# Moving one batch's transposes from TensorE to the DMA crossbar in a sparse attention and MLP kernel

## The chip, the cores and the metric

The kernel runs on one core of a Trainium2 chip. The metric is device time in microseconds (us) of one execution. A run whose time is over 1.5% above the fastest of the same kernel is called slow, and "faster" or "slower" is said from 2% on. A ratio below is the mean time of one kernel's fast runs over that of the other's fast runs of the same rounds, so it is not quite the ratio of the medians that are quoted beside it. Intervals are 95%.

## The reference, cut to what matters

Eight batches of eight heads, 576 positions, 64 columns. Heads 0 to 3 see a window of 32 positions ("local"), heads 4 to 7 every 32nd position ("strided"). The attention output is the input of a two-layer network, 4608 tokens by 512, then 2048, then 512.

```python
mask_local   = (rel >= 0) & (rel < stride)
mask_strided = (rel >= 0) & (pos[None, :] % stride == pos[:, None] % stride)
...                                    # softmax(q k^T / 8) v for each head
h = x @ w_in
g = np.where(h > 0.0, h, np.exp(np.minimum(h, 0.0)) - 1.0)
return g @ w_out
```

## The kernel before

Scores need q and k with the 64 columns across partitions, so both are transposed. Two ways are in the kernel: TensorE against an identity matrix, with a copy out of PSUM after it (`piece_T`), or a DMA crossbar transpose queued on SyncE (`dma_T`). Before, batches 0 to 2 go the first way, batches 3 to 7 the second.

```python
def piece_T(b, hp, engs=None, wide=True):       # TensorE way
    ...
                nc.tensor.transpose(o, x, identity[0:n, 0:n])
    for i, (dst, blk) in enumerate(both):
        copy(engs[i] if engs else nc.vector, dst, ps[i])

def dma_T(b, which):                            # crossbar way
    ...
    nc.sync.dma_start_transpose(out=out_.rearrange("p (c n) -> p c n", n=n), in_=in_)
```

There is one pair of source tiles `qs`, `ks` for the strided heads of every batch: loads of the next batch wait until this batch is transposed. All loads but the first four, of batch 0, stand in GpSimd's queue, and the output stores in SyncE's.

After two blocks of layer 1, a hand-written order interleaves batch 1's attention with layer 2 groups (four matmuls each, `2` in the string). Then a loop over the remaining layer 1 groups carries everything else. `SC` says at which step each head pair's scores come; `u` is a half of it.

```python
for it in ("2 S4 2 S5 2 2 B4 S6 2 E4 A5 S7 2 E5 B6 2 E6 A7 2 E7 v "
           "T0 2 S0 S1 2 T1 k B0 2 E0 S2 2 A1 E1 S3 2 B2 E2 2 A3 2 E3 t 2 x").split():
    ...      # S scores, A/B probability times v, E its tail, T TensorE transposes of batch 1,
             # t those of batch 2's strided heads, v k x loads
for b in range(3, B):
    st = int(SC[b][0])
    ...
    at(st - (3 if b == 3 else 4), lambda b=b: Ts(b))          # crossbar, four tiles
for n, (j, t) in enumerate(L1S):
    for f in jobs.pop(n, []): f()
    l2_to(n + 10)
    for f in jobs.pop(n + .5, []): f()
    l1(j, t, mode="B" if n < 18 and n % 3 == 0 else "A")
```

The softmax here doesn't subtract the row's maximum and nothing guards it: scores larger than these inputs give would overflow.

## Time and profile before

| | before |
|---|---|
| time, median of the 4 runs beside the changed kernel | 324.17 us (323.82 to 325.11) |
| span of the profiled run | 322.6 us |
| TensorE idle from 24.78 to 94.72 us | 4.2 us |
| TensorE idle from 94.72 to 300 us | 0.14 us |

The page's first lines, the table of stretches and the rows of the timeline are shown and read in the prediction.

### The profile page before, as it was taken

How to read it: one execution, taken by the hardware profiler on the slowest of the kernel's cores; microseconds unless marked ns; L12 is line 12 of the kernel's file. 1: busy time of each engine (PE TensorE's matmuls, PEld its weight loads, DVE VectorE, ACT ScalarE, POOL GpSimd, SP SyncE). 2: the span in 40 equal slices, each digit the busy share in tenths (PEclk: the TensorE clock that was granted, in tenths of full speed). 3: DMA queues.
4: the chain of work that ended last, by engine and by line, in shares of the span. 5: the costliest groups of instructions: out<-in, count | busy, mean ns of one | idle time of the engine just before them, and what ended most of it. 6: DMA issues, size and time to landing. Idle time of an engine off the chain costs nothing.

```text
span 322.6 us, 7819 instructions
## 1 busy us (share of the span) xinstructions
PE 310.8 (96%) x2992; PEld 223.6 (69%) x2992; DVE 239.5 (74%) x485; ACT 220.2 (68%) x429; POOL 115.6 (36%) x162
## 2 busy tenths in 40 slices
PE   7898998989999999999999999999999999999994
PEld 5658953577667777777777777777777777777763
DVE  7664973477667888888888988898888866666660
ACT  3697766677688888777777777778888643443431
POOL 6352368788046903790259125920000000000000
PEclk9999999999999999999999999999999999999999
DMA  8999999999499949993999599969211111111112
GB/s 160 191 205 207 208 151 142 153 147 129 52 143 182 122 70 155 172 141 64 137 158 161 70 136 167 149 77 169 57 35 35 34 35 33 34 35 49 51 33 65
DMA packets 113990, 36.36 MB, mean 113 GB/s; under 512 B 101154, under 2 KB 107458, under 8 KB 113954
## 3 DMA queue, kind: packets, MB, share of 16 engines
q0 software_dynamic: 79696, 18.87, 61.3%
q1 hardware_dynamic: 32766, 16.28, 24.6%
q10 hardware_dynamic: 1492, 0.74, 1.0%
q8 instruction: 23, 0.38, 0.5%
q14 instruction: 13, 0.11, 0.1%
HBM read 38.04 MB, written 9.44 MB: 147 GB/s over the span
## 4 chain that ended last, share of the span: by engine, by line
PE 83%; DVE 6%; ACT 5%; DMA 3%; issue 1%; SPq 0%; DVEq 0%; ACTq 0%
PE ops L463 36%; PE hps L406 33%; PE sc L293 4%; PE ox L345 3%; DVE g L421 2%; DMA kl<-in_k_dram 2%; DMA ksT<-ks 1%; PE idle L487 1%; DVE g L440 1%; PE opl L478 1%; PE tp L270 1%; DVE he L420 1%; ACT vsx L528 1%; ACT big L437 1%; ACT e L296 1%
## 5 line engine op out<-in xcount | busy, mean ns | idle before, releaser
L463 PE MATMUL ops<-w_out_sb,g 128*128 128x512 bf16 x560 | 143.6, 380 | 0.1
L406 PE MATMUL hps<-xT,w_in_sb 128*128 128x256 bf16 x1088 | 140.7, 273 | 1.3 <-DVE g L421 1.3
L406 PEld LDWEIGHTS <-w_in_sb 128*128 128x128 bf16 x1088 | 117.3, 114 | 23.6 <-issue 1.5
L413 ACT ACTIVATE he<-hps 128x512 f32<-128x512 f32 x136 | 80.2, 593 | 52.3 <-PE hps L406 50.0
L421 DVE TENSOR_TENSOR g<-he,hps 128x512 bf16<-128x512 bf16 x130 | 89.4, 687 | 13.6
L463 PEld LDWEIGHTS <-g 128*128 128x128 bf16 x560 | 50.4, 98 | 37.2 <-DVE g L421 0.3
L420 DVE TENSOR_SCALAR he<-he 128x512 bf16<-128x512 f32 x130 | 57.7, 444 | 20.9 <-ACT he L413 19.5
L296 ACT ACTIVATE e<-sc 128x576 bf16<-128x576 f32 (+1 forms) x64 | 38.5, 645 | 4.6 <-PE sc L293 4.6
L468 ACT COPY osb<-ops 128x512 f32<-128x512 f32 x35 | 20.5, 587 | 12.3 <-PE ops L463 9.4
L143 POOL DMA_DIRECT2D qs<-in_q_dram x8 | 6.2, 774 | 48.9 <-DMA qsT<-qs 47.5
L348 ACT ACTIVATE ln<-ox 64x288 f32<-64x288 f32 x40 | 16.3, 409 | 10.7 <-PE ox L345 10.1
L125 POOL DMA_DIRECT2D klb<-in_k_dram x28 | 20.7, 747 | 7.9 <-DMA w_in_sb<-in_moe_w_in_dram 5.2
L133 POOL DMA_DIRECT2D vlx<-in_v_dram x28 | 21.9, 782 | 4.1 <-DMA w_out_sb<-in_moe_w_out_dram 1.9
L313 DVE TENSOR_TENSOR xT<-ox,rc 64x288 bf16<-64x288 f32 x40 | 18.1, 453 | 5.7 <-ACT rc L351 5.4
L317 DVE TENSOR_TENSOR xT<-ox,rc 64x288 bf16<-64x288 f32 x40 | 18.1, 453 | 5.5 <-ACT rc L351 5.1
L119 POOL DMA_DIRECT2D qlb<-in_q_dram x20 | 16.6, 833 | 13.8 <-DMA ks<-in_k_dram 10.0
L134 POOL DMA_DIRECT2D vlx<-in_v_dram x28 | 17.3, 618 | 4.2 <-DMA qlb<-in_q_dram 2.1
L351 ACT ACTIVATE rc<-ln 128x288 f32<-128x288 f32 x40 | 17.7, 443 | 1.3
L138 POOL DMA_DIRECT2D vsx<-in_v_dram x20 | 16.2, 816 | 0.9 <-DMA klb<-in_k_dram 0.9
L349 ACT ACTIVATE ln<-ox 64x288 f32<-64x288 f32 x40 | 16.1, 403 | 0.5
L304 DVE TENSOR_TENSOR pm<-e,mask_l 128x576 bf16<-128x576 bf16 x32 | 13.5, 453 | 3.3 <-ACT e L296 3.0
L487 PE MATMUL idle<-warm 128*128 128x256 bf16 x92 | 14.3, 299 | 1.3 <-DVE warm L182 1.3
(101 smaller groups left out, 243.2 us busy)
## 6 DMA issues: line engine op xcount, KB each, us to landing
out_dram<-osb SPq DMA_DIRECT2D x31, 144.0 KB
qs<-in_q_dram POOLq DMA_DIRECT2D x8, 288.0 KB, 6.4
ks<-in_k_dram POOLq DMA_DIRECT2D x8, 288.0 KB, 8.7
w_in_sb<-in_moe_w_in_dram POOLq DMA_DIRECT2D x2, 1024.0 KB, 17.0
w_out_sb<-in_moe_w_out_dram POOLq DMA_DIRECT2D x4, 512.0 KB, 15.7
klb<-in_k_dram POOLq DMA_DIRECT2D x28, 72.0 KB, 8.2
vlx<-in_v_dram POOLq DMA_DIRECT2D x28, 72.0 KB, 3.6
qlb<-in_q_dram POOLq DMA_DIRECT2D x20, 72.0 KB, 7.0
```

What stands on the lines that cost most here:

```text
L125: nc.gpsimd.dma_start(out=klb[b % 2][:, h // 2, :, (h % 2) * D:(h % 2 + 1) * D], in_=k[b, h].rearrange("(t p) d -> p t d", p=LQ))
L133: nc.gpsimd.dma_start(out=t[PRE:128], in_=x)
L296: nc.scalar.activation(e[0:R], sc[0:R, :, 0:W], ACT.Exp, scale=scale)
L313: nc.vector.tensor_mul(xs[:, u * W:(u + 1) * W], o[pr], rc[pr])
L317: nc.vector.tensor_mul(dst, o[pr].rearrange(pat, b=3, s=NS), rc[pr].rearrange(pat, b=3, s=NS))
L351: nc.scalar.activation(rc, ln, ACT.Exp, scale=-1.0)
L406: nc.tensor.matmul(hps[:, mm], lhsT=w_in_of(m, c), rhs=xT[:, c, r0:r0 + SUB], start=(c == 0), stop=(c == KC - 1))
L413: nc.scalar.activation(e, hps, ACT.Exp)
L420: eng.tensor_scalar(e1, e, scalar1=1.0, scalar2=1.0, op0=ALU.min, op1=ALU.subtract)
L421: nc.vector.tensor_tensor(gt, e1, hps, op=ALU.max)
L463: nc.tensor.matmul(ops, lhsT=g[:, m, kk * 128:(kk + 1) * 128], rhs=w_out_sb[:, m, :], start=(m == 0), stop=(m == MC - 1))
L468: nc.scalar.copy(o_sb, ops)
```

## The change

The intent is to spare TensorE all transposes of batch 2 and to close three waits in batch 1's attention. The core of the diff:

```diff
     def load_ql16(b):
-        if b < 3:
-            nc.gpsimd.dma_start(out=qld[b % 2][0:RS], ...)     # one load, halves apart
-            return
         for h in range(HG):                                    # four small loads
...
+    for i in range(2):                 # now at the empty start
+        one_columns(i)
     load_str(0, qs, q)
...
     def pitch(b):
-        return RS if b < 3 else RP
+        return RS if b < 2 else RP
...
-    one_columns(1)
     load_str(1, qs, q)
...
     load_str(2, ks, k)
-    load_kl16(2)
-    load_ql16(2)
-    load_vl16(2)
...
-    for it in ("2 S4 2 S5 2 2 B4 S6 2 E4 A5 S7 2 E5 B6 2 E6 A7 2 E7 v "
-               "T0 2 S0 S1 2 T1 k B0 2 E0 S2 2 A1 E1 S3 2 B2 E2 2 A3 2 E3 t 2 x").split():
+    for it in ("2 S4 2 S5 2 2 B4 S6 2 E4 A5 S7 2 E5 B6 2 E6 T0 2 t A7 v E7 S0 2 T1 S1 2 k B0 2 E0 S2 2 A1 E1 S3 t B2 2 "
+               "E2 A3 E3 x").split():
...
         elif it == "v":
             load_str(2, vs, v)
+            load_kl16(2)
+            load_ql16(2)
+            load_vl16(2)
         elif it == "k":
+            load_str(3, qs, q)
+            load_str(3, ks, k)
+            load_vsx16(3)
             load_kl16(3)
             load_ql16(3)
-            load_vsx16(3)
         elif it == "t":
-            for p in (2, 3):
-                piece_T(2, p)
+            Ts(2, *(("qs", "ks") if l2n[0] < 10 else ("kl", "ql")))
...
-            piece_T(1, n, (nc.vector, nc.scalar))
+            piece_T(1, n, (nc.vector, nc.scalar if n else nc.vector))
...
-    SC = {2: (2.5, 5.5, 9, 12), }
+    SC = {2: (4.5, 7.5, 10, 12.5), }
...
-    for p, n in ((0, 8), (1, 10)):
-        at(n, lambda p=p: do(("TT", 2, p)))
...
-        l2_to(n + 10)
+        l2_to(max(n + 10, min(13 + (n + 2) // 2, 16)))
```

Three layer 2 groups that stood ahead of the loop now stand in its first steps.

More of the change, by code (lines that the diff above doesn't have):

```diff
@@ L78 @@
     qlb = [const([RP, 2, NS, 2 * D], BF16, f"qlb{i}") for i in range(2)]
-    qld = [t.rearrange("p a s c -> p (a s c)").rearrange("p (h c) -> p h c", h=HG) for t in qlb]
     klb = [const([LQ, 2, LB, 2 * D], BF16, f"klb{i}") for i in range(2)]
@@ L113, in load_ql16 @@
     def load_ql16(b):
-        if b < 3:
-            nc.gpsimd.dma_start(out=qld[b % 2][0:RS],
-                                in_=q[b, 0:HG].rearrange("h (p s) d -> p h (s d)", s=NS))
-            return
         for h in range(HG):
@@ L182 @@
     nc.vector.memset(warm, 1.0)
+    nc.vector.memset(vlx[1][0:PRE, :, 0, :], 0.0)
     nc.vector.memset(identity, 1.0)
@@ L190, with one_columns @@
     )
+    def one_columns(i):
+        for t in (vlx[i], vsx[i]):
+            o = t.rearrange("p a t (y d) -> p (a t) y d", d=D)[:, :, 1, :]
+            nc.scalar.copy(o, warm[0:o.shape[0], 0:D].unsqueeze(1).to_broadcast(o.shape))
+    for i in range(2):
+        one_columns(i)
     load_str(0, qs, q)
@@ L243, in t_parts @@
             dst = qlT[i][:, a * 8 * n:(a + 1) * 8 * n]
-            blk = ([qlb[i][0:n, a, j] for j in range(NS)] if b not in (1, 2) else
-                   [[qld[i][0:n, 2 * a + x, j * D:(j + 1) * D] for x in range(2)]
-                    for j in range(NS)])
+            blk = [qlb[i][0:n, a, j] for j in range(NS)]
         else:
@@ L265, in piece_T @@
                 o = ps[i][:, j * n:(j + 1) * n]
-                if type(x) is list:
-                    for z in range(2):
-                        nc.tensor.transpose(o[z * D:(z + 1) * D], x[z], identity[0:n, 0:n])
-                else:
-                    nc.tensor.transpose(o, x, identity[0:n, 0:n])
+                nc.tensor.transpose(o, x, identity[0:n, 0:n])
         for i, (dst, blk) in enumerate(both):
@@ L524 @@
     P = [(p, u) for p in range(4) for u in range(2)]
-    def one_columns(i):
-        for t in (vlx[i], vsx[i]):
-            o = t.rearrange("p a t (y d) -> p (a t) y d", d=D)[:, :, 1, :]
-            nc.scalar.copy(o, warm[0:o.shape[0], 0:D].unsqueeze(1).to_broadcast(o.shape))
-    for it in ("f7 S0 S1 1 f6 T1 f6 S2 S3 m f8 T2 T3q T3k f3 S4 S5 f3 S6 S7 M4 f3 E4 M5 f3 E5 M6 f3 E6 "
+    for it in ("f7 S0 S1 f6 T1 f6 S2 S3 m f8 T2 T3q T3k f3 S4 S5 f3 S6 S7 M4 f3 E4 M5 f3 E5 M6 f3 E6 "
                "v M7 f3 E7 M0 f3 E0 M1 f3 E1 M2 f3 E2 M3 f12 E3").split():
@@ L536 @@
             spins(n)
-        elif it == "1":
-            one_columns(0)
         elif it == "v":
@@ L557 @@
     nc.vector.memset(qlb[1][64:RP], 0.0)
-    nc.vector.memset(vlx[1][0:PRE, :, 0, :], 0.0)
-    one_columns(1)
     load_str(1, qs, q)
@@ L600, in l2_to, with Ts @@
             l2n[0] += 1
-    for it in ("2 S4 2 S5 2 2 B4 S6 2 E4 A5 S7 2 E5 B6 2 E6 A7 2 E7 v "
-               "T0 2 S0 S1 2 T1 k B0 2 E0 S2 2 A1 E1 S3 2 B2 E2 2 A3 2 E3 t 2 x").split():
+    def Ts(b, *names):
+        for w in names:
+            dma_T(b, w)
+    for it in ("2 S4 2 S5 2 2 B4 S6 2 E4 A5 S7 2 E5 B6 2 E6 T0 2 t A7 v E7 S0 2 T1 S1 2 k B0 2 E0 S2 2 A1 E1 S3 t B2 2 "
+               "E2 A3 E3 x").split():
         n = int(it[-1]) if it[-1].isdigit() else 0
@@ L608 @@
             load_str(2, vs, v)
+            load_kl16(2)
+            load_ql16(2)
+            load_vl16(2)
         elif it == "k":
+            load_str(3, qs, q)
+            load_str(3, ks, k)
+            load_vsx16(3)
             load_kl16(3)
             load_ql16(3)
-            load_vsx16(3)
         elif it == "t":
-            for p in (2, 3):
-                piece_T(2, p)
+            Ts(2, *(("qs", "ks") if l2n[0] < 10 else ("kl", "ql")))
         elif it == "x":
-            load_str(3, qs, q)
-            load_str(3, ks, k)
             load_vl16(3)
         elif it[0] == "T":
-            piece_T(1, n, (nc.vector, nc.scalar))
+            piece_T(1, n, (nc.vector, nc.scalar if n else nc.vector))
         elif it[0] in "AB":
@@ L630, in at @@
         jobs.setdefault(int(2 * n) / 2, []).extend(its)
-    def Ts(b):
-        for w in ("qs", "ks", "kl", "ql"):
-            dma_T(b, w)
-    SC = {2: (2.5, 5.5, 9, 12), }
+    SC = {2: (4.5, 7.5, 10, 12.5), }
     SC.update({b: tuple(15 + 16 * (b - 3) + 4 * i for i in range(4)) for b in range(3, B)})
-    for p, n in ((0, 8), (1, 10)):
-        at(n, lambda p=p: do(("TT", 2, p)))
     for b in range(3, B):
@@ L646 @@
                                      load_ql16(b), load_vsx16(b), load_vl16(b)))
-        at(st - (3 if b == 3 else 4), lambda b=b: Ts(b))
+        at(st - (3 if b == 3 else 4), lambda b=b: Ts(b, "qs", "ks", "kl", "ql"))
     for b in range(2, B):
```

## The prediction

> **What bounds the kernel now.** I read the page first, then busy time by stretch, then the timeline of TensorE from 24 to 125 us, then those of ScalarE, VectorE, GpSimd and SyncE at each hole. The page and the table of stretches:
>
> ```profile
> span 322.6 us, 7819 instructions
> PE 310.8 (96%) x2992; PEld 223.6 (69%) x2992; DVE 239.5 (74%) x485; ACT 220.2 (68%) x429; POOL 115.6 (36%) x162
> PE 83%; DVE 6%; ACT 5%; DMA 3%; issue 1%; SPq 0%; DVEq 0%; ACTq 0%
> ```
>
> ```profile
> 24.78:41.57 16.79, 15.46 (x163) 15.02 (x161) 11.81 (x21) 12.66 (x17) 5.01 (x7) 1.00 1.18 207
> 41.57:65.90 24.33, 22.79 (x270) 11.53 (x268) 13.14 (x29) 14.87 (x31) 19.13 (x28) 1.00 1.37 145
> 65.90:94.72 28.82, 27.52 (x317) 19.27 (x316) 20.11 (x42) 22.38 (x45) 13.48 (x19) 1.00 1.16 119
> 94.72:300.00 205.28, 205.14 (x1840) 149.63 (x1839) 167.64 (x333) 147.16 (x295) 64.60 (x87) 1.00 0.81 99
> ```
>
> The columns are the stretch, its length, and busy time of PE, PEld, DVE, ACT and POOL. From 94.72 us TensorE lacks 0.14 us in 205: everything later is one unbroken queue of matmuls. So the end moves by what TensorE does not have to do, or wait for, before 95 us, and by nothing else. Its holes before 95 us add up to 4.2 us (1.33 + 1.54 + 1.30, length less busy). The change works between 24 and 90 us. The rows of the timeline that carry the sum (start, length, engine, line, operation):
>
> ```profile
> 26.40 0.83 ACT L528 COPY vlx<-warm 128x768 bf16<-128x768 bf16 x1 [2.01 <-DVE vlx L558]
> 27.14 1.04 ACT L528 COPY vsx<-warm 72x1024 bf16<-72x1024 bf16 x1
> 28.09 1.02 ACT L437 ACTIVATE big<-hpw 128x1024 f32<-128x1024 f32 x1
> 32.49 1.03 PE L406 MATMUL hps<-xT,w_in_sb 128*128 128x256 bf16 x8 [1.32 <-DVE g L421]
> ...
> 51.90 0.45 PE L268 MATMUL tp<-identity,qlb 72*64 72x72 bf16 x16
> 52.28 0.43 PE L270 MATMUL tp<-identity,klb 96*128 96x96 bf16 x6
> 54.96 0.43 PE L293 MATMUL sc<-qlT,klT 64*128 64x96 bf16 x12 [1.30 <-ACT klT L253]
> ...
> 63.85 0.43 PE L270 MATMUL tp<-identity,qs 72*128 72x72 bf16 x8
> 65.03 1.03 PE L463 MATMUL ops<-w_out_sb,g 128*128 128x512 bf16 x4
> 71.83 0.31 PE L368 MATMUL so<-pm,ones 72*64 72x288 bf16 x2 [1.05 <-DVE pm L298]
> 77.45 1.06 PE L406 MATMUL hps<-xT,w_in_sb 128*128 128x256 bf16 x8
> 78.44 0.45 PE L268 MATMUL tp<-identity,qlb 72*64 72x72 bf16 x16
> 79.09 1.03 PE L463 MATMUL ops<-w_out_sb,g 128*128 128x512 bf16 x4
> ```
>
> Read starts, not lengths: the lengths overlap. The strided transposes of batch 2 hold TensorE from 63.85 to 65.03, one local piece from 78.44 to 79.09.
>
> **What the Trainium skill says.** "TensorE: Matmul & The Clock Gate", section "Back-to-back issue gap", puts 512 columns at about 216 ns on a warm clock when isolated, and fewer in a stream. Here four such matmuls start every 0.87 us (63.85 less 62.98), 217 ns each, at a granted clock of 1.00: the tail is at that rate, and TensorE's instruction count is the lever. The same page, "Part 4: PE-mode transpose", says that a transpose ends in PSUM and needs a copy after it, and took about 275 ns in one kernel. The trace shows 198 ns for one but starts 33 ns apart (eight in 0.26 us), so I count 33 ns; the copies show as 450 ns on VectorE and 639 ns on ScalarE. "DMA: Bandwidth & Descriptors", section "DMA Transpose (X-bar)", asks for a partition dimension that is a multiple of 16 and for issue from SyncE or ScalarE. That is why batch 2 goes to rows padded from 72 to 80 and to four small query loads in place of one. Its section "Issuing engines are not separate DMA queues" says that all transfers share 16 engines and interleave. The trace agrees as far as it goes: the mean share of the DMA engines is 1.3 to 1.6 over 48 to 80 us, while GpSimd loads.
>
> **The change part by part.**
>
> (a) The columns of ones for batch 1 leave ScalarE's path at 26.40 and go, with batch 0's, to the empty start: four copies, 1.66 us per pair by starts, after the table load ends at 2.08, so done at about 5.4; ScalarE's first needed work starts at 6.07. The first wide exponential then starts when its matmuls are in, about 26.7 in place of 28.09. The VectorE result that TensorE awaits at 32.49 comes 1.39 us sooner, so that wait of 1.32 us goes. I take off 0.1 for a 0.22 us memset that now stands ahead of the first loads. Gain 1.2.
>
> (b) Batch 1's local query transposes: 16 half blocks become 8 whole ones, twice. 0.38 us becomes 0.26: gain 0.24.
>
> (c) They move ahead of the last strided P v, with both first copies on VectorE ahead of a reciprocal product. The ScalarE copy that TensorE awaited 1.30 us then lies behind other work. Gain 1.30.
>
> (d) Batch 2's strided transposes go: 65.03 - 63.85 = 1.18. Its two local pieces: from the layer 1 group's start to the next layer 2 group was 79.09 - 77.45 = 1.64 us, and without them such a step takes 0.87, so 0.77 each, 1.54, and a wait of 0.20 behind the first. Gain 2.92.
>
> (e) The wait of 1.05 at 71.83: probabilities come late from VectorE because layer 1 steps follow each other without layer 2 between. Three layer 2 groups now move from before the loop into it, so VectorE is less behind when these scores come. By the durations (score to exponential 0.35, exponential 0.65, then a layer 1 pair of 1.1 us ahead of the second mask product) some 0.6 us stays. Gain 0.45.
>
> (f) What is lost: fewer layer 2 groups fill batch 1's attention. A product waits for ScalarE and VectorE to free its PSUM tile ahead of the second local transposes, about 0.35; the last local P v waits for its mask product, about 0.6; the first layer 1 step of the loop now has 0.9 us of work in place of 2.9 us in front, while reciprocal and product take 1.4 (63.09 to 64.47), about 0.6. Loss 1.55.
>
> Sum: 1.2 + 0.24 + 1.30 + 2.92 + 0.45 - 1.55 = 4.6 us. VectorE also loses eight copies (3.6 us) but bounds nothing later, so I count nothing for it.
>
> **Are the crossbar's results in time?**
>
> ```profile
> 47.05 0.59 POOL L134 DMA_DIRECT2D vlx<-in_v_dram  x1 [0.40 <-DMA qlb<-in_q_dram]
> 87.31 1.47 SPq L169 DMA_TRANSPOSE qsT<-qs  x1
> 88.89 1.88 SPq L169 DMA_TRANSPOSE ksT<-ks  x1
> 92.92 0.75 POOL L143 DMA_DIRECT2D qs<-in_q_dram  x1 [11.92 <-DMA qsT<-qs]
> ```
>
> GpSimd's queue reuses eight completion semaphores, so each load waits for the eighth before it. The single batch 1 query load was in by 47.05. The four small ones end at about 44, and those for the first piece are the first two; I need them at 49.2 (51.90 less 1.2 of (a) and 1.35 of moving ahead). Batch 2's strided q and k are then issued near 49.5 to 51, against 47.84 before, and land at about 55.5 and 57 (k took 5.9 us before: issued by 49.29, landed by 55.17). A crossbar transpose took at most 5.6 us from issue until the reload of its source began (87.31 to 92.92), so the key transpose is through at about 62.5 on quiet queues. TensorE wants it at step 4.5, by my count at 67 us: about 61.5 for the loop's start, then five layer 1 steps at 0.9 and two layer 2 groups. The reserve of 4 us must cover that this time the local loads of batch 2 run beside the transposes. I take 0.3 us for the chance that it does not. The local transposes are wanted at step 10, near 79 us, and are in by about 72.
>
> **The rivals.**
>
> Rival 1, the crossbar comes late: its loads queue behind the small query loads, transposes and loads share the engines, and TensorE stops at the first batch 2 score. For it: the DMA share above 1.3 and a key load that starts 1.7 us later. Against it: the two extra steps and the 4 us reserve. If the transposes take twice as long, TensorE stops for 1 to 3 us: 320.5 to 323.
>
> Rival 2, the holes only move. The parts of (f) grow, because TensorE waits on the same ScalarE and VectorE chain with less filler. For it: two waits of over a microsecond in this stretch that are such chains. Against it: the transposes are 3 us of TensorE work that nobody must do again. If none of (c) and (e) is kept: 321.5.
>
> Rival 3, all parts hold and (f) costs nothing, as the order was surely tried: 318.2. Even that is just short of 2%.
>
> Rival 4, the earlier layer 1 runs into the output weights. Their last quarter lands near 43.2 (the eighth load after it starts then); the layer 2 group that needs it stood at 44.84 and moves to 43.6. At most 0.3 us is lost.
>
> **Range and chances.** 324.4 - 4.6 + 0.3 is 320.1 us. The terms of (f) are worked out from queues one after the other and are rather too large than too small, and rival 3 lies below, so I lean 0.4 us towards it: 319.7 us, a gain of 1.4%. The range: 318.2 where (f) is free, 321.8 where rival 1 or 2 takes half of the gain. 2% faster is 317.9, beyond the sum of all gains, so 8%; slower by 2% needs stops of 11 us, 1%.
>
> **What would show it.** Right: TensorE's matmul count falls by 92 to 2900 (32 strided, 44 local in batch 2, 16 in batch 1); no wait on VectorE's g near 31; none of 1.3 us on klT; the loop's first layer 1 step near 61.5; small new waits before it; the first batch 2 score with no wait on the transposes. From step 16 on everything equal but 4 to 5 us earlier. Wrong: a wait on qsT or ksT at that score (rival 1), or holes before 95 us that again add up to 4 us (rival 2), or a hole after 95 us, which would mean that a later load or store came late.

## The result, and the profile after

The changed kernel took 321.44 us in the median of four runs: 321.09, 321.26 and 321.62, and one slow run of 326.04. The kernel before took 324.17 beside it. The ratio is 0.9908 (0.9879 to 0.9936), a gain of 0.9%. It lies inside the predicted range, 1.7 us above the predicted 319.7.

The page of the changed kernel (span; busy time, share and instructions; then the chain of work that ended last, by engine):

```profile
span 319.9 us, 7608 instructions
PE 304.7 (95%) x2857; PEld 221.5 (69%) x2900; DVE 237.7 (74%) x478; ACT 219.5 (69%) x428; POOL 121.2 (38%) x168
PE 85%; DMA 8%; DVE 3%; ACT 2%; issue 2%; DVEq 0%; ACTq 0%
```

Weight loads fell from 2992 to 2900, the 92 that were foretold. (The matmul records are 2857 because some are missing from this trace; that is also why the last row below seems to lack 1.7 us.) The DMA's share of the chain went from 3% to 8%. The same four stretches:

```profile
24.78:41.57 16.79, 16.67 (x170) 15.56 (x171) 12.96 (x20) 11.79 (x16) 5.12 (x7) 1.00 1.17 207
41.57:65.90 24.33, 22.31 (x238) 12.98 (x242) 13.20 (x29) 15.17 (x32) 16.92 (x24) 1.00 1.48 141
65.90:94.72 28.82, 25.48 (x275) 16.95 (x277) 19.80 (x40) 22.78 (x46) 21.15 (x30) 1.00 1.70 172
94.72:300.00 205.28, 203.55 (x1797) 149.80 (x1828) 166.51 (x331) 145.87 (x293) 65.00 (x86) 1.00 0.81 98
```

The first stretch is nearly closed: TensorE lacks 0.12 us where it lacked 1.33. The second lacks 2.02 (before 1.54), the third 3.34 (before 1.30). The DMA share, second from the right, is the summed time of all DMA packets over the time of the core's 16 engines, and can exceed 1 when packets overlap. It rose from 1.37 to 1.48 and from 1.16 to 1.70. Where TensorE waits, in its timeline, with the wait before the group in brackets (the line by itself is batch 3's first score in the kernel before):

```profile
53.24 0.42 PE L267 MATMUL tp<-identity,qlb 72*128 72x72 bf16 x8 [0.26 <-DVE xT L310]
...
60.15 0.31 PE L371 MATMUL so<-pm,ones 128*64 128x288 bf16 x2 [0.55 <-DVE pm L301]
...
62.06 1.80 PE L403 MATMUL hps<-xT,w_in_sb 128*128 128x256 bf16 x15 [0.39 <-DVE xT L314]
...
67.99 0.30 PE L290 MATMUL sc<-qsT,ksT 64*128 64x72 bf16 x8 [0.65 <-DMA ksT<-ks]
...
71.60 0.31 PE L365 MATMUL so<-pm,ones 72*64 72x288 bf16 x2 [0.71 <-DVE pm L295]
...
93.39 0.43 PE L290 MATMUL sc<-qsT,ksT 64*128 64x72 bf16 x16 [1.45 <-DMA ksT<-ks]
```

```profile
95.69 0.47 PE L293 MATMUL sc<-qsT,ksT 64*128 64x72 bf16 x16
```

The three small waits on VectorE (0.26, 0.55, 0.39) are the ones that the prediction named, and the wait at 71.60 has shrunk as it said. What it did not count are the two waits on the transposed strided key: 0.65 at batch 2's first score, 1.45 at batch 3's. Together they are 2.1 us. Batch 3's is the odd one, since batch 3 went through the crossbar in both kernels. Its first score was at 95.69 before and is at 93.39 now, 2.30 us earlier; taking the two waits off, by subtraction, it would be 4.40 earlier.

SyncE's queue shows why batch 3 is late (issue start, time spent on issuing), and below it the copy on ScalarE whose result the last stores of the group write out:

```profile
57.31 4.64 SPq L164 DMA_TRANSPOSE ksT<-ks  x1
...
71.73 11.55 SPq L448 DMA_DIRECT2D out_dram<-osb  x5
83.45 3.42 SPq L164 DMA_TRANSPOSE qsT<-qs  x1
86.97 2.38 SPq L164 DMA_TRANSPOSE ksT<-ks  x1
```

```profile
81.46 0.61 ACT L465 COPY osb<-ops 128x512 f32<-128x512 f32 x1
```

And GpSimd's, whose wait for an earlier load tells when that load had landed:

```profile
80.10 0.72 POOL L120 DMA_DIRECT2D klb<-in_k_dram  x1 [1.01 <-DMA ks<-in_k_dram]
```

Batch 3's strided key was in the core at about 80.1, its query at about 78.3. The transposes were issued from 83.45 on, right behind a group of output stores. SyncE took its queue in order, and the last two of those five stores write a layer 2 result that ScalarE copied out only from 81.46 to 82.07. Behind that, the key's transpose needs 6.4 us from its issue at 86.97 to the score at 93.39, at a time when GpSimd still loads batch 3's local tiles (until 89.4; before, the loads of this batch ended at about 81). In the kernel before, these transposes stood behind stores too (issued from 87.31, their data in by 80.4), but the key's was through within 5.3 us (88.89 to 94.19) and TensorE came to the score only at 95.69.

So two theories are to be tested. The **contention theory** says that the crossbar is slow because loads run beside it. The **queue theory** says that the transposes are issued late, behind stores. The rivals to both are that the small VectorE waits matter more, or that the parts interact in another way.

### The profile page after: what moved, and what is told of

It is laid out like the page before. It is cut to its first block, busy times and chain, and to the rows that moved or that the text cites.

```text
span 319.9 us, 7608 instructions
## 1 busy us (share of the span) xinstructions
PE 304.7 (95%) x2857; PEld 221.5 (69%) x2900; DVE 237.7 (74%) x478; ACT 219.5 (69%) x428; POOL 121.2 (38%) x168
## 4 chain that ended last, share of the span: by engine, by line
PE 85%; DMA 8%; DVE 3%; ACT 2%; issue 2%; DVEq 0%; ACTq 0%
PE ops L460 35%; PE hps L403 35%; DMA ksT<-ks 5%; PE sc L290 4%; PE ox L342 3%; DMA kl<-in_k_dram 2%; PE idle L484 2%; PE hpw L428 2%; PE opl L475 1%; PE tp L267 1%; DVE g L418 1%; PE o_ps L375 1%; PE s_ps L365 0%; PE s_ps L371 0%; DVE g L437 0%
## 5 line engine op out<-in xcount | busy, mean ns | idle before, releaser
L460 PE MATMUL ops<-w_out_sb,g 128*128 128x512 bf16 x517 | 137.1, 380 | 2.5 <-issue 0.6
L418 DVE TENSOR_TENSOR g<-he,hps 128x512 bf16<-128x512 bf16 x130 | 89.4, 688 | 13.9 <-PE hps L403 0.5
L114 POOL DMA_DIRECT2D qlb<-in_q_dram x28 | 23.1, 830 | 16.8 <-DMA ks<-in_k_dram 8.3
L120 POOL DMA_DIRECT2D klb<-in_k_dram x28 | 21.4, 776 | 10.8 <-DMA w_in_sb<-in_moe_w_in_dram 5.8
L128 POOL DMA_DIRECT2D vlx<-in_v_dram x28 | 22.1, 789 | 2.1 <-DMA klb<-in_k_dram 1.2
L129 POOL DMA_DIRECT2D vlx<-in_v_dram x28 | 17.8, 637 | 1.3 <-DMA klb<-in_k_dram 1.0
L295 DVE TENSOR_TENSOR pm<-e,mask_s 72x576 bf16<-72x576 bf16 x32 | 13.6, 450 | 3.8 <-ACT e L293 3.5
```

The lines of the kernel that those rows point to most:

```text
L114: nc.gpsimd.dma_start(out=qlb[b % 2][0:RS, h // 2, :, (h % 2) * D:(h % 2 + 1) * D], in_=q[b, h].rearrange("(p s) d -> p s d", s=NS))
L120: nc.gpsimd.dma_start(out=klb[b % 2][:, h // 2, :, (h % 2) * D:(h % 2 + 1) * D], in_=k[b, h].rearrange("(t p) d -> p t d", p=LQ))
L128: nc.gpsimd.dma_start(out=t[PRE:128], in_=x)
L418: nc.vector.tensor_tensor(gt, e1, hps, op=ALU.max)
L460: nc.tensor.matmul(ops, lhsT=g[:, m, kk * 128:(kk + 1) * 128], rhs=w_out_sb[:, m, :], start=(m == 0), stop=(m == MC - 1))
```

## The experiments

Eleven kernels ran, in three calls. Beside them the kernel before had medians of 324.47, 324.44 and 324.73 us (11, 11 and 7 runs). Kernels are compared only within the same rounds. Each profile is one run; a slow run is left out of the ratio, but not out of the median.

### Batch 2's local loads taken away (wrong result)

```diff
             load_str(2, vs, v)
-            load_kl16(2)
-            load_ql16(2)
-            load_vl16(2)
```

> The changed kernel without the 16 loads of batch 2's local q, k and v (wrong result on purpose: old data is used). Theory, contention: the crossbar transposes of batch 2 and 3 came late because loads of small rows share the 16 DMA engines with them. Then the key transpose of batch 2 takes at most 5.5 us from issue to the score instead of 10.6, both waits on ksT (0.65 and 1.45 us) go, and the time falls by 2.1 to about 319.2 us. Rival, serial queue: the transposes are late because SyncE issues them one after the other behind stores and behind the landing of ks; then the 10.6 us and the first wait stay, and the time is 320.5 or more.

It took 319.93 us, ratio 0.986 (0.984 to 0.9879). Both waits on the key are gone. The key's transpose of batch 2 and the load that then overwrites its source, in this kernel:

```profile
56.75 3.06 SPq L164 DMA_TRANSPOSE ksT<-ks  x1
...
62.47 0.71 POOL L138 DMA_DIRECT2D ks<-in_k_dram  x1 [0.47 <-issue]
```

The transpose was through within 5.7 us of its issue; in the changed kernel it was 10.7 (57.31 to 67.99). The stretch of 57 to 68 us, first in the changed kernel, then in this one:

```profile
57.00:68.00 11.00, 9.36 (x83) 6.17 (x82) 5.49 (x11) 7.53 (x16) 4.84 (x8) 1.00 1.72 162
```

```profile
57.00:68.00 11.00, 10.06 (x96) 7.03 (x94) 6.14 (x11) 7.54 (x17) 6.24 (x9) 1.00 1.15 174
```

The DMA share is 1.15 in place of 1.72 while the engines move no less (174 against 162 GB/s). Contention holds for batch 2. The gain was 1.5 us and not 2.1, since at the second half of batch 3's first scores a wait of 0.36 on the attention output shows up, which the key's wait had covered.

### Batch 3's local v loads later

```diff
         elif it == "x":
-            load_vl16(3)
+            pass
...
-            at(st - 13, lambda b=b: (load_str(b, qs, q), load_str(b, ks, k), load_kl16(b),
+            at(st - 13, lambda b=b: (load_str(b, qs, q), load_str(b, ks, k),
+                                     load_vl16(3) if b == 4 else None, load_kl16(b),
```

> The changed kernel with batch 3's local v loads put behind the reload of qs and ks for batch 4, so that GpSimd can't issue them beside batch 3's strided transposes. Contention: the wait of 1.45 us on ksT at batch 3's first score falls to 0.3 or less, the one of 0.65 at batch 2's stays, time about 320.0 us. Rival, issued too late whatever runs beside: 1.45 stays, 321.3 us.

320.8 us, ratio 0.9897 (0.9874 to 0.992). Batch 3's wait on the key is gone (0.35 on the attention output is left), but the loads of batch 4 now come later and a wait of the same kind is there one batch on. The issue of batch 3's key transpose, and that wait:

```profile
84.98 3.06 SPq L164 DMA_TRANSPOSE ksT<-ks  x1
...
124.15 0.43 PE L290 MATMUL sc<-qsT,ksT 64*128 64x72 bf16 x16 [0.87 <-DMA ksT<-ks]
```

Postponing the load handed the wait on. Is it contention at batch 3 too? The key's transpose was through within 5.9 us of its issue here, when TensorE came to the score at 90.88; with the v loads beside it it took 6.4 in the changed kernel and 7.8, 8.3 and 8.6 in three others below. That speaks for it. But it was also issued 2.0 us sooner than in the changed kernel (84.98 against 86.97), so this run does not tell the two theories apart.

### Batch 3's transposes one step earlier

```diff
-        at(st - (3 if b == 3 else 4), lambda b=b: Ts(b, "qs", "ks", "kl", "ql"))
+        at(st - 4, lambda b=b: Ts(b, "qs", "ks", "kl", "ql"))
```

> The changed kernel with batch 3's four crossbar transposes issued at step 11 in place of 12, one step of some 2 us earlier, as the later batches have it. If lead time is what lacks: the wait of 1.45 us goes, time about 320.0 us. If the DMA engines are full and the transposes only meet more loads (ks of batch 3 landed near 80 us, where step 11 stands): the wait shrinks by less than half, 320.7 us or more.

The edit did nothing: the order of instructions on each engine is the same as in the changed kernel, because the store of step 10 still stands ahead. It is a repeat of the changed kernel, then: 323.26 us in the median of six, one of them slow, ratio 0.9945 (0.9911 to 0.9979). Its profiled run waits 0.97 and 1.85 us on the key. The repeat is useful: it says how far the same program strays (0.9908 and 0.9945 with overlapping intervals), and that the two waits vary from run to run. Nor is the clock behind all of it: the profiled run, at 322.91, had a granted clock of 1.000.

### The columns of ones alone, on the kernel before

```diff
+    nc.vector.memset(vlx[1][0:PRE, :, 0, :], 0.0)     # ahead of the first loads
+    for i in range(2):
+        one_columns(i)
     load_str(0, qs, q)
...
-    nc.vector.memset(vlx[1][0:PRE, :, 0, :], 0.0)
-    one_columns(1)
```

> The kernel before with part (a) alone: all columns of ones written by ScalarE in the empty start. Prediction's term: 1.2 us gained; by the trace of the changed kernel 1.0 (the layer 1 group after the wait stands at 32.34 in place of 33.36). So about 323.2 us, with no wait on VectorE's g at 32 us. Rival, the gain is lost again because the output weights or the batch 1 loads are then waited for: 324.2 us, with a new wait between 40 and 50 us.

324.23 us with one of six runs slow, ratio 0.9977 (0.9943 to 1.0011): not resolved. In the trace part (a) is there: the score that stood at 54.96 us stands at 53.95, 1.0 us earlier. Then the run loses it again. The wait on the probabilities, and a row of the stretches after it (the third number from the right is the granted clock):

```profile
71.15 0.31 PE L376 MATMUL so<-pm,ones 72*64 72x288 bf16 x2 [1.29 <-DVE pm L306]
```

```profile
73.00:75.00 2.00, 2.00 (x17) 1.31 (x16) 1.03 (x3) 1.13 (x2) 2.00 (x4) 0.50 0.96 106
```

Behind the hole the granted clock was 0.70 in 71 to 73 us, 0.50 in the next two and 0.94 in the two after, which costs an estimated 1.7 us: 0.6 + 1.0 + 0.1 of those six. A hole can cost more than its own length. The two runs with a clock of 1.000 throughout took 323.10 and 322.39 us, so part (a) may well be worth its microsecond where the clock holds; two runs are too few to say so.

### Batch 3's strided transposes ahead of the stores

```diff
-        at(st - (3 if b == 3 else 4), lambda b=b: Ts(b, "qs", "ks", "kl", "ql"))
+        if b == 3:
+            at(st - 5, lambda b=b: Ts(b, "qs", "ks"))
+            at(st - 3, lambda b=b: Ts(b, "kl", "ql"))
+        else:
+            at(st - 4, lambda b=b: Ts(b, "qs", "ks", "kl", "ql"))
```

> The changed kernel with batch 3's two strided transposes issued at step 10, now ahead of the output stores of that step in SyncE's queue (the run that moved them to step 11 changed no instruction's place: the last store before them is that of step 10). Serial queue, at batch 3: the transpose of qs then starts when qs has landed, about 78.5 us in place of 83.5, the wait on ksT at batch 3's first score goes, about 0.35 us of wait on an xT product stays behind it, and the time falls by 1.1 to about 320.1 us. Contention alone: they start earlier but are not done earlier than 91 us because the loads of ql and vl run beside them; the wait shrinks by less than half and the time stays above 320.8 us.

320.6 us, six fast runs between 319.89 and 321.45, ratio 0.9879 (0.9855 to 0.9903). In SyncE's queue, and at the second half of batch 3's first scores on TensorE (the first half starts at 90.88 without a wait):

```profile
77.39 1.71 SPq L164 DMA_TRANSPOSE qsT<-qs  x1
79.23 4.20 SPq L164 DMA_TRANSPOSE ksT<-ks  x1
```

```profile
91.54 0.31 PE L290 MATMUL sc<-qsT,ksT 64*128 64x72 bf16 x8 [0.35 <-DVE xT L314]
```

The transposes are issued six to eight microseconds sooner, as soon as their data is in, and the wait on the key is gone, with every load where it was in its queue. The queue theory holds for batch 3: given the start that they could have had, the transposes were in time with the loads beside them, and so they were in the three later kernels with this edit. How long they took does not show, only that it was under 11.7 us (79.23 to 90.88). One thing moved along: the batch's v loads were issued until 92.3 in place of 89.4, and that this helped is not excluded.

### Batch 2's first scores half a step later

```diff
-    SC = {2: (4.5, 7.5, 10, 12.5), }
+    SC = {2: (5, 7.5, 10, 12.5), }
```

> The changed kernel with batch 2's first strided scores half a step later (step 5 in place of 4.5, the next at 7.5, 10, 12.5 as they were). The wait on ksT at batch 2's first score (0.16 to 0.97 us in three profiles of this schedule) goes, since a layer 1 step of 1.0 us now stands before it, and the wait of 0.7 us for the second mask product goes, since a layer 1 step now parts the two P v. The wait at batch 3's first score is free to take it back: the transposes of batch 3 are tied to the loads, not to TensorE. If they are, it grows from 1.45 to about 2.5 and the time stays at 321.2 us; if they shift along with TensorE, the time falls to 320.2 us. I expect the first, as batch 3's transposes wait for a store that waits for TensorE but have little slack: 320.8 us.

322.51 us, ratio 0.994 (0.9908 to 0.9971): a miss. The wait at batch 2 fell to 0.18, the one on the probabilities stayed (0.76, where it was to go), and at batch 3's first score there is now:

```profile
94.04 0.43 PE L290 MATMUL sc<-qsT,ksT 64*128 64x72 bf16 x16 [2.68 <-DMA ksT<-ks]
```

Again the clock fell after the hole: 0.67, 0.50 and 0.98 in the three pairs of microseconds from 94 on, about 1.7 us lost by the same estimate. TensorE came to this score 0.6 us sooner than in the changed kernel (91.36 against 91.94 without the waits), while the transpose took 8.6 us from its issue at 85.41 in place of 6.4. The hole that was closed at batch 2 opened again at batch 3, behind the same store.

### Both edits

The two diffs above together.

> Both edits: batch 3's strided transposes ahead of step 10's store and batch 2's scores half a step later. If the two waits on ksT and the wait on the second mask product are what the change lost, all of them go and about 0.35 us comes back as a wait on an xT product: 319.2 us, 1.6% under the kernel before. If the DMA engines simply have too much to do in this stretch, a wait on ksT of over a microsecond stays and the time is 320.5 us.

320.75 us, ratio 0.9877 (0.9855 to 0.9899), no better than the early transposes alone. In the profiled run the key was late at batch 2 all the same (1.18 us; 10.2 us from issue to score). The wait on the probabilities is gone in this run, though: probably the late key gave VectorE the time. Half a step is about 1.0 us, and the time from issue to score varies by more: from 9.2 to 10.7 us over the six runs that show a wait there with the same loads.

### Batch 2's local queries in one wide load

One load with rows of 2 KB in place of four with rows of 256 bytes. The values come to lie in the wrong order; it passed the comparison since scores are tiny here (the reference draws q and k at a tenth of a unit normal).

```diff
+        if b == 2:
+            nc.gpsimd.dma_start(out=..., in_=q[b, 0:HG].rearrange("h (p s) d -> p h (s d)", s=NS))
+            return
         for h in range(HG):
```

> The changed kernel with batch 2's local q in one load of 2 KB rows in place of four of 256 byte rows (wrong result on purpose: the rows' order doesn't fit the transpose). If the small rows that the crossbar's layout needs are what slows the key transpose of batch 2, it takes 8 us or less from issue to score in place of 10.6, its wait goes, later loads move up by 2 us or more, and the time is about 320.4 us. If it is the amount of loads at large (k and v are in small rows in both kernels), the 10.6 us fall by less than 1.5 and the time stays at 321.2.

326.14 us with one of six runs slow, ratio 1.0043 (1.0 to 1.0087), the slowest of all:

```profile
71.27 0.30 PE L296 MATMUL sc<-qsT,ksT 64*128 64x72 bf16 x8 [4.20 <-DMA ksT<-ks]
```

The key's transpose took 12.9 us (issued at 58.40), and the clock was halved after the hole. The small rows of the query loads are not needed for a slow transpose. That they have no part in it is not shown, since the edit moved another thing: with three fewer instructions in GpSimd's queue, the v loads start at 56.19 in place of 62.49, into the transposes. That how much is in flight beside them counts is the likely reading, and was not tested apart.

### The three layer 2 groups back ahead of the loop

```diff
-    "... A1 E1 S3 t B2 2 E2 A3 E3 x"
+    "... A1 E1 S3 t 2 B2 2 E2 2 A3 2 E3 x"
```

> The changed kernel with the three layer 2 groups ahead of the loop, where they stood before the change. Theory (my sum, parts e and f): they fill the gaps of batch 1's attention, so the small waits there (0.55 on the mask product, 0.39 on the context) fall to under 0.3 together and the wait of 0.71 at the first batch 2 product grows to 1.0 or so; the wait on the strided key stays. Time within 0.6 us of the changed kernel: 321.0, ratio 0.990. Rival: without the groups between them the first steps of the loop run VectorE behind, and the holes in 66 to 80 us grow by over 1 us: 322.5, ratio 0.994.

324.77 us, ratio 0.9999 (0.9958 to 1.0041): the rival was right that time is lost, and by more than it said, but not at the place that it named. The wait at the first batch 2 product is 0.95, as my own sum had it. The waits of 0.55 and 0.39 are gone, but in the loop:

```profile
64.22 3.54 PE L403 MATMUL hps<-xT,w_in_sb 128*128 128x256 bf16 x31 [1.84 <-DVE xT L314]
```

TensorE comes to the loop's layer 1 with nothing to do beside it and waits 1.84 us for the attention output that is its input, where it waited 0.39. At batch 3's first score the key's wait is 2.52, and the clock falls to 0.58 and 0.56 for four microseconds after it. The clock is not all of it: the one run with a granted clock of 1.000 still took 324.17 us.

### Early transposes, and the groups ahead of the loop

The diff of the early transposes and that of the groups together.

> Both: batch 3's strided transposes ahead of the stores, and the three layer 2 groups ahead of the loop. If the two edits are independent: the ratio of the first kernel of this call less 0.0025 (the early transposes alone measured 0.9879 against 0.9908). 320.2 us, ratio 0.9875. If the groups' place also sets when the output stores stand in SyncE's queue, the transposes of batch 3 are issued at another time than 77.4 us, and a wait of over 0.5 us is back.

321.78 us, ratio 0.9899 (0.9862 to 0.9935). The second half of batch 3's first scores here:

```profile
93.76 0.31 PE L290 MATMUL sc<-qsT,ksT 64*128 64x72 bf16 x8 [0.35 <-DVE xT L314]
```

This is the clean measure of the groups, since neither this trace nor that of the early transposes alone has a wait on the key at batch 3 or a halved clock: from the second local transposes of batch 1 (53.58) to this score (93.76) it is 40.18 us, in the kernel with the early transposes alone 38.90 (52.64 to 91.54). Moving the groups into the loop is worth about 1.3 us by these two traces; the intervals of the two ratios overlap. The two edits are not additive, in the good direction: the groups' kernel alone (0.9999) loses 0.01 by the late key and the clock after it, and nearly all of this comes back when the transposes are early.

### Early transposes, and batch 2's local v loads later

```diff
             load_ql16(2)
-            load_vl16(2)
         elif it == "k":
             load_str(3, qs, q)
             load_str(3, ks, k)
+            load_vl16(2)
```

> The kernel with batch 3's strided transposes ahead of the output stores, and in addition batch 2's eight local v loads issued behind batch 3's strided q and k. Result stays correct. Contention theory: with the v loads gone from 57 to 66 us the strided key transpose of batch 2 takes under 8 us from issue to score (9 to 12.8 in every run with them) and the share of the DMA engines there falls below 1.4; no wait on it at batch 2's first score, none over 0.4 at batch 3's. 320.3 us, ratio 0.987; that is at most 0.3 below the kernel without the move. Rival (it is the local key and query loads, or the output stores, that slow it): 9 us or more and the wait as before. Second rival: the v loads now run beside batch 3's transposes, and the wait moves there: over 0.5 us.

321.65 us, ratio 0.9926 (0.9866 to 0.9987), one of four runs at 324.39; not told apart from its base. The size that I expected fell: no v load is left in 57 to 66 us, yet the DMA share there is still 1.64 to 1.75, and the transposes are no faster. The load that overwrites the source of the query's transpose (issued at 54.92) waits as long as this:

```profile
64.80 0.72 POOL L138 DMA_DIRECT2D qs<-in_q_dram  x1 [4.00 <-DMA qsT<-qs]
```

That is 9.9 us, against 6.1 in the kernel without any local loads (55.17 to 61.29). What these two traces leave as the difference is the local k and q loads, issued at 53 to 61 us: they hold up batch 2's transposes here. The score shows no wait in this run only because TensorE reached it at 67.82, some 1.1 us later than in its base (67.01 less a wait of 0.27). Which of the k and the q loads it is, was not tried.

## Why the prediction was right or wrong

The range held; the middle was 1.7 us too low. The step that failed is the prediction's answer to "Are the crossbar's results in time?": a key transpose of at most 5.6 us with a reserve of 4 us, and 0.3 us for the chance that this does not do. The key's transpose of batch 2 took 10.7 us, and the waits on the key measured 2.1 us. Both of its own signs of being wrong appeared: a wait on ksT at batch 2's first score, and holes of over 4 us before 95 us.

That the time fell inside the range is partly luck. The range reached 321.8 for the case that rival 1 takes half of the gain; the median is 0.4 under that, and the same program repeated (batch 3's transposes one step earlier) came to a ratio of 0.9945, which on the 324.17 measured beside the changed kernel is about 322.4, outside the range. By its own steps:

- **(a), 1.2 us.** Right: the layer 1 group behind the wait starts at 32.34 in place of 33.36, 1.02 us earlier, and the wait on VectorE is gone. Whether the copies at the start cost the 0.1 is lost in the spread: TensorE's wide layer 1 began at 25.14, before at 24.89, and between 24.70 and 25.65 in the other kernels with these copies.
- **(b), (c), (d).** Right: 92 weight loads fewer and no wait on klT.
- **The loop's first layer 1 step near 61.5.** It starts at 61.40 and then waits 0.39. TensorE came to batch 2's first score at 67.34 (67.99 less the wait), close to the 67 of the prediction. The text there says five layer 1 steps before it; the trace has four, and with four its 67 comes out.
- **(e), 0.45 us.** The wait of 1.05 became 0.71, a gain of 0.34 at the place that was named. But this is not what moving the groups is for: with late scores, leaving them ahead of the loop costs about 1.3 us through the wait of 1.84. I did not see that case.
- **(f), a loss of 1.55.** The new waits are 0.26, 0.55 and 0.39, and a wait of 0.18 near 45 us became 0.44: 1.46 in all. The last is not clearly the change's, since it is 0.15 in the kernel with the early transposes; without it the three make 1.20.
- **The sum, 4.6 us.** Taking off the waits on the key it is 4.40 us at batch 3's first score.
- **"I take 0.3 us for the chance that it does not."** This is the term that was too small. It measured 2.1 us in the profiled run, 0.65 at batch 2 and 1.45 at batch 3, and that is rival 1 with its own figure of 1 to 3 us. Two things were behind it. The 5.6 us for a transpose was read from a stretch in which GpSimd loaded nothing, and the reserve of 4 us was taken for safe although loads run beside it now; there it took 9.2 to 10.7 us. And only batch 2's crossbar was looked at: for batch 3 the later loads and the store ahead of the transposes were visible in the queue's order.
- **The lean of 0.4 us towards rival 3** went the wrong way for the same reason.
- **Rival 2** (the holes only move) is true of the hole times: TensorE lacks 5.5 us before 95 us now, 4.2 before. At least 0.6 of the 5.5 is missing records: four gaps of 0.16 with no wait, each before a group that shows three of its four matmuls. It is not true of the parts that it named: (c) and (e) were kept, and what moved in is the wait on the key, beside the losses foretold in (f).
- **Rival 4** (the output weights) did not show: the layer 2 groups at 42.99 run without a wait. In the kernel with both edits one such group waited 0.54 us for them.

The account closes: 4.40 less 2.10 is 2.30 us at batch 3's first score. The medians differ by 2.73 and the spans by 2.7; the 0.4 us that the changed kernel gains after 95 us was not followed.

The key's wait at batch 2 differs, 0.16 to 1.18 us, between runs whose queues are alike. Two spans behind it vary: from the transpose's issue to TensorE's arrival it is 9.0 to 10.4 us, from issue to score 9.2 to 10.7. Why they do is open. The best kernel measured is the one with batch 3's strided transposes ahead of the stores, 320.6 us; its interval (0.9855 to 0.9903) overlaps that of the changed kernel (0.9879 to 0.9936), but its trace shows the removed wait.

## What to carry to other kernels

A duration read from a quiet stretch can be too short for a busy one (here 5.6 us against 9.2 to 10.7): before you move a transfer into a stretch with loads, ask what will be in flight there, and take the longer one for the reserve. When work goes to a DMA queue, read the whole in-order queue that it joins, for this batch and the next: a transpose behind a store starts when the store's data is there, not when its own is. And where several waits lie in a row, closing one lets the engine arrive sooner at the next; give the transfers a head start at all of them before you count the gain.

## What the Trainium skill lacked or had wrong

- "Advanced Engine Details and Errata", section "X-Bar Transpose (TRN2)", says that transposes are as fast as regular DMAs, at 350 to 400 GB/s. The transposes here move 328 KB each (80 x 2048 values of 2 bytes), which at that rate would be under 1 us, an estimate from the page's figure. With batch 2's local loads taken away one was through within 5.7 us of its issue, and with loads beside it batch 2's took 9.2 to 12.9 us. These times run from the issue to the use, not of the bytes alone; the first half of the sentence is not refuted, as a plain load of the key tile took 5.9 us in the kernel before (49.29 to 55.17).
- "DMA: Bandwidth & Descriptors", section "Issuing engines are not separate DMA queues", says that all transfers interleave on the same 16 engines. The runs agree (a share of 1.72 against 1.15, and 10.7 us against 5.7 for the same transpose), but the section gives no size for what a transfer loses by it, and a size is what a reserve needs.
- "TensorE: Matmul & The Clock Gate", section "HAM oscillation", ties the half clock to idle gaps of over about 3.4 us. Here holes of 1.29, 2.52 and 2.68 us were followed by four to six microseconds at a reduced clock, down to 0.50 or 0.56, and ones of 1.30, 1.45 and 1.85 us by none. The page does say that the window is free-running and does not start with the kernel; in these runs gaps well under its figure were enough at times.
